# One PSUM bank for the up products of a delta-rule and feed-forward kernel, emptied by VectorE; two merges placed beside other pieces; last stores from two queues

## The chip, the cores and the metric

The kernel runs on one core of a Trainium2 chip. The metric is the device time of one execution in microseconds (us). Three runs of the kernel before gave 621.1, 622.01 and 622.45 us; the median is 622.01 us. One further execution was profiled: it took 620.85 us by its own timer, and the span from its first to its last instruction is 619.1 us, so 1.75 us lie outside the span.

## The reference

A linear attention with a state that follows the delta rule, over 768 steps for 4 batches of 8 heads of width 48, and then a feed-forward layer with a piecewise activation:

```python
for t in range(S):
    kt, vt, bt = (k_n[:, :, t], v[:, :, t], beta[:, :, t, None])
    y[:, :, t] = np.einsum('bhd,bhde->bhe', q[:, :, t], state)
    v_old = np.einsum('bhde,bhd->bhe', state, kt)
    state = state + bt[:, :, :, None] * np.einsum('bhd,bhe->bhde', kt, vt - v_old)
...
h = x @ w_in
g = np.where(pos, h, np.where(neg, 0.0, (h + beta) ** 2 / (4.0 * beta)))
return (g @ w_out).astype(np.float32)
```

Here x is y with the heads side by side (3072 rows of 384), w_in is 384 x 2048, w_out is 2048 x 384, pos is h >= 1, neg is h <= -1 and beta is 1. So g is h above 1, 0 below -1, and a parabola between.

## The kernel before

**Tiling.** The 768 steps are cut into 12 chunks of 64, and two chunks of all four batches make a pair, G = 0 to 5, of 512 rows. Inside a chunk the delta rule is solved as a triangular system, and the state is carried from chunk to chunk. The feed-forward layer of a pair runs over 16 blocks f of 128 hidden units. One block of one pair is an *item*. Pair 0 is split further, so there are 102 items: 22 for pair 0, and 16 for each of the pairs 1 to 5.

**An item.** `up` (L628 to L637) makes 9 matmuls of 512 columns into a PSUM bank h: three slices of the contraction, each in three passes of high and low parts. The activation then goes over two engines. ScalarE computes relu(0.5 - 0.5 h) out of PSUM into s (L762), relu(1 - s) in place (L762 again, since both go through the helper `relu`) and its square (L789). VectorE takes the maximum of h, still in PSUM, and s (L791). `rest` (L753 to L759) splits s into ghi, a rounded copy by ScalarE (L757), and glo, the remainder, by VectorE (L758). `down` (L639 to L651) makes 12 matmuls of 384 columns into the four banks o0 to o3, two items later.

**PSUM.** The eight banks are two named h, which take turns item by item, two named ch, and o0 to o3. The attention's *pieces*, which are groups of 64 to 128 small matmuls, get their banks from `acc` (L65): in pairs 1 to 5 from the two ch banks alone.

**Order.** The order is written by hand. While the items of pair G run, the attention of pair G+1 is computed between them. `plan` (L687 onward) puts pieces (`pe`) and VectorE work (`fill`) into half-slots: half-slot t of a pair belongs to item floor(t), and a whole number stands just behind that item's `up`, a half one behind the `down` that follows it. Each engine works through its own instructions in exactly the order of the code. In the order of one item: what a piece of the half-slot before still has to move (`finish(late)`), `rest` of the item before, `up`, the first relu, the pieces and fills of the whole slot, `down` of two items earlier, the other ScalarE steps, the pieces of the half slot, the maximum, and the fills of the half slot.

**The attention of a pair.** `gram_k` (L204) and `gram_q` (L217) multiply keys with keys and queries with keys. The result of `gram_q` is masked by three VectorE instructions (L237). `lanes` (L264) transposes the key products and normalizes; GpSimd then masks A (L296). `solve_whole` (L319) inverts 32 x 32 triangles in 30 steps of two VectorE instructions each (L325, L327), which are fills of the items 0 to 7 and of the end of the pair before. `unlanes_whole` (L330) brings the result back (L333, L335, L338). `merge32` (L385) joins two triangles of 32 into one of 64, with matmuls L392 and L394 and six ScalarE copies. `chain_r`, `chain_u`, `chain_y` and `chain_d` (L409 to L513) go through the two chunks in turn and carry the state SU.

In pairs 1 to 4 `chain_r` of the first chunk stands at half-slot 2.5, `gram_q` of the first at 4.5 and of the second at 6, the merges at 8.5, 9 and 11 and the chain from 10 to 15. Pair 5 has no such work beside its items.

**The end.** `store` (L653) copies each bank o to SBUF and issues two DMAs of 96 KB for it; in the last pair ScalarE and VectorE copy in turn, and all but the last of the eight DMAs are issued by the SP queue.

Of the kernel before, what the change touches and what calls it, by code (L numbers as in the profile page):

```python
# [7 lines left out]
F32 = mybir.dt.float32  # L8
F32R = mybir.dt.float32r
I32 = mybir.dt.int32  # L10
AF = mybir.ActivationFunctionType
ALU = mybir.AluOpType

C = 64
NP = 4
D = 48
CT = 2
NV = CT * NP
DM = 384
# [11 lines left out]
def delta_rule_moe(ctx: ExitStack, tc: tile.TileContext, kqa, kqb, kv, beta, w, out):  # L31
# [14 lines left out]
    nc = tc.nc  # L46
    ntot, NT = kv.shape[0], kv.shape[1]
    CB = NT * CT
    NU = CB * NP
    H = NU // 2  # L50
    NB = CB * C
    P = 128
    NS = ntot // 2
    TT = 2 * NB // P

    const = ctx.enter_context(tc.tile_pool(name="const", bufs=1))
    sb = ctx.enter_context(tc.tile_pool(name="sb", bufs=2))
# [1 line left out]
    ctx.enter_context(tc.manual_schedule())  # L59

    K, KE, GE, Q, KV, XB, RAW, WT = {}, {}, {}, {}, {}, {}, {}, {}
    START = [dict(name=n, bufs=b) for n, b in (("ch", 2), ("ch", 2), ("h", 2), ("h", 2), ("o2", 1), ("o3", 1), ("o0", 1), ("o1", 1))]
    spare = []

    def acc():  # L65
# [151 lines left out]
    def gram_q(g):  # L217

        x, b_ = Q[g], banks(C)
        for j in range(H):  # L220
            for e, f in quarters():
                r, o = slice(f * C, f * C + D), other(e, f) * C
                nc.tensor.matmul(b_[e][o:o + C, j], K[g][r, e * H + j, :], x[r, (1 - f, 1)[e], e * H + j, :], start=True, stop=True)  # L223

        def moved():
            for o in range(2):
                yield x[o * C:o * C + C, o, 0:H], b_[0][o * C:o * C + C], slice(o * C, o * C + C)
            yield x[:, 0, H:NU], b_[1], slice(0, P)

        def evict():  # L230
            def raw():
                for a, b, r in moved():
                    nc.scalar.copy(out=a, in_=b)

            def masks(copied=False):
                for a, b, r in moved():
                    nc.vector.tensor_tensor(out=a, in0=a if copied else b, in1=mask[r, None, :].broadcast_to([r.stop - r.start, H, C]), op=ALU.mult)  # L237
                    yield
            return (raw, masks(True)) if g < 2 else lambda: run(masks())
        return evict  # L240
# [373 lines left out]
    oacc, gs = {}, {}  # L614
# [13 lines left out]
        return slice(bs[0] * NB, bs[-1] * NB + NB)  # L628

    def up(G, f, bs):  # L630
        h = ps.tile([P, 2 * NB], F32, name="h", bufs=2)
        n = 0
        for k in range(3):
            for x, y in PASSES:
                nc.tensor.matmul(h[:, cols(bs)], WT[f][:, 0, x, k * P:(k + 1) * P], XB[G][:, y, k, cols(bs)], start=(n == 0), stop=(n == 8))  # L635
                n += 1
        return h  # L637
# [15 lines left out]
    def store(G, b):  # L653
        o = sb.tile([P, 2, DM], F32, name="wx", bufs=2)
        for k in (2 * b, 2 * b + 1):
            (nc.scalar.copy, nc.vector.tensor_copy)[k % 2 if G == NS - 1 else 0](out=o[:, k % 2], in_=oacc[G, k])
            for j in range(CT):
                (nc.scalar if G == NS - 1 and k + j == TT else nc.sync).dma_start(out=out.rearrange("(b n t) m -> n b t m", b=CB, t=C)[2 * G + b, k % 2 * CT + j], in_=o[j * C:j * C + C, k % 2])

    pe, fill = {}, {}  # L660

    def at(where, G, t, *x):
        where.setdefault(2 * first[G] + int(round(2 * t)), []).extend(x)
# [5 lines left out]
    def chain(G, t, a):  # L669
        for j, f, g in ((0, chain_u, a), (0.5, chain_y, a), (1.5, chain_d, a), (2.5, chain_r, a + 1), (3.5, chain_u, a + 1), (4, chain_y, a + 1), (5, chain_d, a + 1)):  # L670
            if (f, g) != (chain_d, ntot - 1):
                at(pe, G, t + j, lambda f=f, g=g: f(g))

    def plan(G):

        a, b = 2 * G + 2, 2 * G + 3
        if G == NS - 1:
            return
        va, vb = scale_v(a), scale_v(b)
        if G == 0:  # L680
            for j, f in ((0, merge16_b), (0.5, chain_r), (1, lambda g: merge32(g, None, True)), (2, lambda g: merge32(None, g)), (3, chain_u), (4, chain_y), (5, chain_d)):
                at(pe, G, j, lambda f=f: f(1))
            back = restore()
            at(fill, G, 0, (sv[1], 2))
            at(fill, G, 1, (load_k, b), (weight_loads, 7, 9), (load_q, a), (weight_loads, 9, 10), (load_kv, a), (weight_loads, 10, 13))
            at(fill, G, 1.5, (back, 1))
            at(fill, G, 2.5, (back, 1), (raws[1][1], 9))  # L687
            for j, n in enumerate((2, 2, 3)):
                at(fill, G, 3.5 + j, (early[0], n))
            at(fill, G, 6.5, (early[1], 1))  # L690
            at(fill, G, 7, (early[1], 9))
            at(fill, G, 4.5, (load_q, b), (weight_loads, 13, 14))
            at(fill, G, 5.5, (load_kv, b), (weight_loads, 14, 15))
            at(fill, G, 8, (load_k, a + 2), (weight_loads, 15, FT))
            for j in range(2):
                at(fill, G, 6 + j / 2, (va, 1))
                at(fill, G, 11.5 + j / 2, (vb, 1))
            at(pe, G, 6, lambda: gram_q(a))
            at(pe, G, 7, lambda: chain_r(a))
            at(pe, G, 11, lambda: gram_q(b))  # L700
            for j, f in ((8, merge16_a), (9.5, merge16_b)):
                for g in range(2):
                    at(pe, G, j + g / 2, lambda f=f, g=g: f(g))
            M = 12.5
            last = FT + HALF
        else:
            so, un = solves.pop(G)
            at(fill, G, 0.5, (va, 1))
            at(fill, G, 1, (va, 1))
            at(pe, G, 2.5, lambda: chain_r(a))  # L710
            at(pe, G, 4.5, lambda: gram_q(a))
            at(pe, G, 6, lambda: gram_q(b))
            cost, hs = 0, 0
            t, n = (-2.5, 19) if G == 1 else (-1.5, 17)
            for j in range(1, 31):
                at(fill, G, t + hs / 2, (so, 1))
                cost += j * (31 - j) + 150
                hs = int(cost / 9461 * n)
            for j, t in enumerate((7, 7.5, 8, 8)):
                at(fill, G, t, (un, 1))  # L720
            at(fill, G, 9, (vb, 1))
            at(fill, G, 9.5, (vb, 1))
            M = 8.5
            last = 16
        for j, x in ((0, (0, None)), (0.5, (1, 0)), (2.5, (None, 1))):
            at(pe, G, M + j, lambda x=x: merge32(*x))
        chain(G, M + 1.5, a)
        if G < NS - 2:
            if G:
                at(fill, G, 6.5, (load_k, a + 2))  # L730
            at(fill, G, M + 0.5, (load_k, b + 2, (nc.sync, nc.sync), True))
            at(pe, G, M + 1, lambda: gram_k(a + 2))
            at(pe, G, M + 3.5, lambda: gram_k(b + 2))
            lane_steps(G, M + 2, lanes(G + 2), 2.5, 3, 3.5, 4)
            solves[G + 1] = solve_whole(), unlanes_whole()
            at(fill, G, M + 3, (load_q, a + 2))
            at(fill, G, M + 5, (load_k, b + 2))
            at(fill, G, M + 6.5, (load_q, b + 2))
            at(fill, G, last + 0.5, (load_kv, a + 2))
            at(fill, G, last + 1.5, (load_kv, b + 2))  # L740
# [20 lines left out]
    def relu(out, in_, bias, scale):  # L761
        nc.scalar.activation(out=out, in_=in_, func=AF.Relu, bias=bias, scale=scale)  # L762

    late, last, ready = [], None, []
    for n, item in enumerate(items):
        at_, c = 2 * n, cols(item[2])
        finish(late)
        if last:
            rest(*last)
            ready.append(last[0])  # L770
        if at_ == 2 * HALF:
            spare.clear()
        h = up(*item)

        s = sb.tile([P, 2 * NB], F32, name="s", bufs=2)
        relu(s[:, c], h[:, c], mid, -0.5)
        evicts = products(*pe.pop(at_, []))
        run(wu, 3 if n == 0 else 1)
        fills(at_)
        finish(evicts)  # L780
        run(wu, 2 if n < HALF else 1)
        if len(ready) == LAG:
            x = ready.pop(0)
            down(*x)
            for b in x[2]:
                if left[x[0], b] == 0:
                    store(x[0], b)
        relu(s[:, c], s[:, c], one, -1.0)
        nc.scalar.activation(out=s[:, c], in_=s[:, c], func=AF.Square)  # L789
        late = products(*pe.pop(at_ + 1, []))  # L790
        nc.vector.tensor_tensor(out=s[:, c], in0=h[:, c], in1=s[:, c], op=ALU.max)  # L791
        run(wu, 2)
        fills(at_ + 1)
        last = item, s
# [3 lines left out]
    for b in range(2):  # L798
        gs[G, FT - 1, (b,)] = gs[G, FT - 1, (0, 1)]
        down(G, FT - 1, (b,))  # L800
        store(G, b)

# [1 line left out]
def layouts(q, k, v, beta, moe_w_in, moe_w_out):  # L804
# [43 lines left out]
```

## Time and profile before

| | |
|---|---|
| median of three runs | 622.01 us |
| profiled execution, its own time | 620.85 us |
| its span | 619.1 us |
| items of pair 1 begin at | 188.9 us |
| items of pair 5 begin at | 541.0 us |
| ScalarE busy | 393.9 us (64%) |
| GpSimd busy | 29.8 us (5%) |
| granted TensorE clock from 120 to 600 us | 1.00 |

The pairs 0 to 4 and the preparation ahead of them fill the first 541 us. From pair 1 on, a pair with attention beside it takes about 90 us, and from the first to the last `up` of pair 5 there are 63 us. In the profile's rows PE is TensorE, DVE is VectorE, ACT is ScalarE, POOL is GpSimd; SPq and ACTq are the DMA issues of the SP and ScalarE queues. A row of the timeline has the start and the duration in us, then engine, line of the code and operation, what is written and read, the sizes, and in brackets how long the engine stood idle before and what ended that.

### The profile page before, as it was taken

The page shows a single profiled execution, that of the slowest core. Times are in us where ns is not written, and L with a number is a line of the kernel's source. Part 1 is how long each engine was busy: PE and PEld are TensorE (multiplying, and loading weights), DVE is VectorE, ACT ScalarE, POOL GpSimd, SP SyncE. Part 2 cuts the span into 40 slices and gives each one's busy share as a digit, 9 for nine tenths or more (in the row PEclk, how much of TensorE's full clock was granted, in tenths as well). Part 3 has the DMA queues.
Part 4 walks back from the last instruction along what each step waited for, and adds up shares of the span by engine and source line. Part 5 has one row for each costly group of instructions (what it writes and reads, how often), then busy time and mean ns, then how long its engine had stood idle before and what let it go on. Part 6 is the DMA issues. An engine that isn't in the chain of part 4 may idle for free.

```text
span 619.1 us, 21754 instructions
## 1 busy us (share of the span) xinstructions
PE 583.6 (94%) x9562; PEld 511.5 (83%) x9562; DVE 409.3 (66%) x848; ACT 393.9 (64%) x685; POOL 29.8 (5%) x62
## 2 busy tenths in 40 slices
PE   7977967799999999999999999999999999999996
PEld 7966956688888888888888888888888888889995
DVE  4989899972379873379973489954489945333332
ACT  3436775649667569656578646587647586666663
POOL 5110000010010000020000020000020000000000
PEclk9556697999999999999999999999999999999999
DMA  5672756200124210214210224110124000020002
GB/s 141 197 244 71 233 196 202 88 4 3 42 61 119 74 31 3 69 31 125 72 30 8 65 53 119 54 31 24 49 71 124 1 4 16 12 54 1 0 1 51
DMA packets 32831, 42.97 MB, mean 69 GB/s; under 512 B 7152, under 2 KB 27440, under 8 KB 32736
## 3 DMA queue, kind: packets, MB, share of 16 engines
q1 hardware_dynamic: 31600, 39.43, 22.6%
q10 hardware_dynamic: 880, 2.07, 1.0%
q8 instruction: 75, 1.23, 0.8%
q0 software_dynamic: 256, 0.08, 0.1%
q14 instruction: 20, 0.16, 0.1%
HBM read 34.47 MB, written 4.72 MB: 63 GB/s over the span
## 4 chain that ended last, share of the span: by engine, by line
PE 70%; ACT 11%; DVE 9%; SPq 3%; DMA 3%; issue 2%; DVEq 0%; ACTq 0%
PE o L650 27%; PE h L635 27%; PE ch L452 3%; ACT XT L406 2%; ACT GG L404 2%; PE ch L414 2%; ACT s L762 2%; PE ch L223 2%; PE ch L430 1%; ACT XT L399 1%; PE ch L496 1%; PE o L583 1%; PE ch L375 1%; ACT s L789 1%; SPq L484 1%
## 5 line engine op out<-in xcount | busy, mean ns | idle before, releaser
L635 PE MATMUL h<-xb,wt 128*128 128x512 f32 (+1 forms) x918 | 229.1, 395 | 9.1 <-DMA xb<-wt 8.1
L635 PEld LDWEIGHTS h<-xb,wt 128*128 128x128 f32 x918 | 166.8, 195 | 43.2 <-DVE xb L183 4.4
L650 PE MATMUL o<-wt,ghi 128*128 128x384 f32 x768 | 202.1, 344 | 0.1
L791 DVE TENSOR_TENSOR s<-h,s 128x512 f32<-128x512 f32 (+1 forms) x102 | 66.8, 655 | 124.3 <-ACT s L789 123.8
L650 PEld LDWEIGHTS o<-wt,ghi 128*128 128x128 f32 x768 | 137.8, 189 | 7.5 <-issue 0.5
L757 ACT CAST ghi<-s 128x512 fp32r<-128x512 f32 (+1 forms) x102 | 60.8, 597 | 110.4 <-DVE s L791 86.3
L650 PE MATMUL o<-wt,glo 128*128 128x384 f32 x384 | 130.3, 339 | 0.4 <-DVE glo L758 0.3
L762 ACT ACTIVATE s<-h,half 128x512 f32<-128x512 f32 (+1 forms) x102 | 67.5, 662 | 44.6 <-PE h L635 43.7
L758 DVE TENSOR_TENSOR glo<-s,ghi 128x512 fp32r<-128x512 f32 (+1 forms) x102 | 66.6, 653 | 34.9 <-ACT ghi L757 34.8
L650 PEld LDWEIGHTS o<-wt,glo 128*128 128x128 f32 x384 | 72.7, 189 | 1.0 <-DVE glo L758 1.0
L762 ACT ACTIVATE s<-s,one 128x512 f32<-128x512 f32 (+1 forms) x102 | 71.7, 703 | 2.4
L789 ACT ACTIVATE s<-s 128x512 f32<-128x512 f32 (+1 forms) x102 | 61.9, 607 | 3.2
L325 DVE TENSOR_TENSOR pr<-A 128x30 f32<-128x30 f32 (+14 forms) x120 | 39.3, 328 | 6.2 <-POOL A L296 4.5
L327 DVE TENSOR_TENSOR A<-A,pr 128x30 f32<-128x30 f32 (+14 forms) x120 | 39.9, 332 | 4.4
L452 PEld LDWEIGHTS ch<-Q,SU 64*64 64x64 f32 (+1 forms) x1008 | 22.1, 135 | 4.3 <-ACT ghi L757 1.5
L452 PE MATMUL ch<-Q,SU 64*64 64x64 f32 (+1 forms) x1008 | 24.3, 222 | 0.7 <-ACT SU L434 0.7
L237 DVE TENSOR_TENSOR Q<-ch,mask 64x512 f32<-64x512 f32 (+1 forms) x30 | 20.6, 688 | 0.4
L296 POOL TENSOR_SCALAR_AFFINE_SELECT A<-A 128x1024 f32<-128x1024 f32 x4 | 5.1, 1263 | 311.9 <-DMA xb<-X 258.1
L404 ACT ACTIVATE GG<-ch 32x512 f32<-32x512 f32 x22 | 13.0, 589 | 10.6 <-PE ch L392 10.3
L414 PEld LDWEIGHTS ch<-SU,K 48*64 48x64 f32 x672 | 13.2, 147 | 6.5 <-issue 4.6
L414 PE MATMUL ch<-SU,K 48*64 48x48 f32 x672 | 14.9, 232 | 3.7 <-DVE Q L237 3.7
L179 ACT ACTIVATE xb<-wt 128x768 f32<-128x768 f32 x16 | 14.5, 914 | 5.1 <-DVE wt L191 3.6
(150 smaller groups left out, 621.8 us busy)
## 6 DMA issues: line engine op xcount, KB each, us to landing
wt<-in_w_dram SPq DMA_DIRECT2D x14, 768.0 KB, 5.4
out_dram<-wx SPq DMA_DIRECT2D x47, 96.0 KB, 2.2
KV<-in_kv_dram SPq DMA_DIRECT2D x36, 96.0 KB, 2.5
KV<-in_kv_dram SPq DMA_DIRECT2D x72, 48.0 KB, 2.4
KV<-in_kv_dram SPq DMA_DIRECT2D x12, 192.0 KB, 2.7
xb<-X SPq DMA_DIRECT2D x60, 32.0 KB, 2.0
K<-in_kqb_dram SPq DMA_DIRECT2D x12, 128.0 KB, 2.7
Q<-in_kqb_dram SPq DMA_DIRECT2D x12, 128.0 KB, 2.7
```

The costliest lines, as they stand in the source:

```text
L325: nc.vector.tensor_tensor(out=pr, in0=A[:, 0:n, j:j + 1].broadcast_to([P, n, m]), in1=A[:, j:j + 1, j + 1:32].broadcast_to([P, n, m]), op= ...
L327: nc.vector.tensor_tensor(out=A[:, 0:n, j + 1:32], in0=A[:, 0:n, j + 1:32], in1=pr, op=ALU.add)
L404: nc.scalar.mul(out=GG[r:r + 32, ga, :, 0:32], in_=y1[r:r + 32], mul=-1.0)
L414: nc.tensor.matmul(b_[f][o:o + C, j], K[g][r, k, :], SU[r, (1 - f, 1)[e], k, :], start=True, stop=True)
L452: nc.tensor.matmul(yy[i][o * C:o * C + C, e, p], SF[rows, u:u + C], w_[rows, x, k, :], **how)
L635: nc.tensor.matmul(h[:, cols(bs)], WT[f][:, 0, x, k * P:(k + 1) * P], XB[G][:, y, k, cols(bs)], start=(n == 0), stop=(n == 8))
L650: nc.tensor.matmul(oacc[G, k], (ghi, glo)[x][:, k * P:(k + 1) * P], WT[f][:, 1, y, :], start=(new and n == 0), stop=(left[G, b] == 0 and n ...
L757: nc.scalar.copy(out=ghi[:, c], in_=s[:, c])
L758: nc.vector.tensor_tensor(out=glo[:, c], in0=s[:, c], in1=ghi[:, c], op=ALU.subtract)
L762: nc.scalar.activation(out=out, in_=in_, func=AF.Relu, bias=bias, scale=scale)
L789: nc.scalar.activation(out=s[:, c], in_=s[:, c], func=AF.Square)
L791: nc.vector.tensor_tensor(out=s[:, c], in0=h[:, c], in1=s[:, c], op=ALU.max)
```

## The change

Up to pair 0 all stays as it was, apart from the banks' names: h becomes h0 and h1. From pair 1 on `up` writes to h0 alone. VectorE at once moves max(h, -1) into s in SBUF, a new instruction (L792 of the new code). ScalarE then computes q = relu(0.5 - 0.5 s) and (1 - q) squared, two steps in place of three, and the maximum (L815) reads s and q from SBUF. For s = max(h, -1) the value 0.5 - 0.5 s never exceeds 1, so that the second relu isn't needed. From item 2 of pair 1 on, the bank h1 is a third bank for the pieces.

`gram_q` of the second chunk goes from half-slot 6 to 8.5, behind the first merge. The last merge goes from 11 to 10.5, ahead of `chain_y`. In the last pair the eight stores are issued by the SP queue and the ScalarE queue, four each.

```diff
     def up(G, f, bs):
-        h = ps.tile([P, 2 * NB], F32, name="h", bufs=2)
+        h = ps.tile([P, 2 * NB], F32, name="h0" if G else f"h{f % 2}")
...
+    def send(G, k, j, o, q):
+        q.dma_start(out=out.rearrange("(b n t) m -> n b t m", b=CB, t=C)[2 * G + k // 2, k % 2 * CT + j], in_=o[j * C:j * C + C, k % 2])
+
+    def store_last(G):
+        o = [sb.tile([P, 2, DM], F32, name="wx", bufs=2) for _ in range(2)]
+        for k in range(TT + 1):
+            if k < TT:
+                (nc.scalar.copy, nc.vector.tensor_copy)[k % 2](out=o[k // 2][:, k % 2], in_=oacc[G, k])
+                send(G, k, 0, o[k // 2], nc.sync)
+            for x in ((0,), (), (1,), (), (2, 3))[k]:
+                send(G, x, 1, o[x // 2], nc.scalar)
...
             at(pe, G, 4.5, lambda: gram_q(a))
-            at(pe, G, 6, lambda: gram_q(b))
...
-        for j, x in ((0, (0, None)), (0.5, (1, 0)), (2.5, (None, 1))):
+        for j, x in ((0, (0, None)), (0.5, (1, 0)), (2 if G else 2.5, (None, 1))):
             at(pe, G, M + j, lambda x=x: merge32(*x))
+        if G:
+            at(pe, G, M, lambda: gram_q(b))
...
+        if item[:2] == (1, 2):
+            spare[:] = START[0:2] + [dict(name="h1", bufs=1)]
         h = up(*item)
 
         s = sb.tile([P, 2 * NB], F32, name="s", bufs=2)
-        relu(s[:, c], h[:, c], mid, -0.5)
+        if item[0]:
+            nc.vector.tensor_scalar(out=s, in0=h, scalar1=-1.0, scalar2=None, op0=ALU.max)
+            q = sb.tile([P, 2 * NB], F32, name="A16", bufs=1)
+            relu(q, s, mid, -0.5)
+        else:
+            relu(s[:, c], h[:, c], mid, -0.5)
...
-        relu(s[:, c], s[:, c], one, -1.0)
-        nc.scalar.activation(out=s[:, c], in_=s[:, c], func=AF.Square)
+        if item[0]:
+            nc.scalar.activation(out=q, in_=q, func=AF.Square, bias=one, scale=-1.0)
+        else:
+            relu(s[:, c], s[:, c], one, -1.0)
+            nc.scalar.activation(out=s[:, c], in_=s[:, c], func=AF.Square)
         late = products(*pe.pop(at_ + 1, []))
-        nc.vector.tensor_tensor(out=s[:, c], in0=h[:, c], in1=s[:, c], op=ALU.max)
+        if item[0]:
+            nc.vector.tensor_tensor(out=s, in0=s, in1=q, op=ALU.max)
+        else:
+            nc.vector.tensor_tensor(out=s[:, c], in0=h[:, c], in1=s[:, c], op=ALU.max)
```

**VectorE, pair 3, from glo of item 5 to glo of item 6.** Line, operation, what is written and read, and the size; glo belongs to the item before the one whose fills follow it. Before:

```order
L758 TENSOR_TENSOR glo<-s,ghi 128x512
L325 TENSOR_TENSOR pr<-A 128x108
L327 TENSOR_TENSOR A<-A,pr 128x27x4
L325 TENSOR_TENSOR pr<-A 128x84
L327 TENSOR_TENSOR A<-A,pr 128x28x3
L237 TENSOR_TENSOR Q<-ch,mask 64x512 x2
L237 TENSOR_TENSOR Q<-ch,mask 128x512
L791 TENSOR_TENSOR s<-h,s 128x512
L325 TENSOR_TENSOR pr<-A 128x58
L327 TENSOR_TENSOR A<-A,pr 128x29x2
L325 TENSOR_TENSOR pr<-A 128x30
L327 TENSOR_TENSOR A<-A,pr 128x30
```

The same place now (L771 is glo, L792 the new move, L815 the maximum, A_6189 is q):

```order
L771 TENSOR_TENSOR glo<-s,ghi 128x512
L792 TENSOR_SCALAR s<-h_6177 128x512
L325 TENSOR_TENSOR pr<-A 128x108
L327 TENSOR_TENSOR A<-A,pr 128x27x4
L325 TENSOR_TENSOR pr<-A 128x84
L327 TENSOR_TENSOR A<-A,pr 128x28x3
L815 TENSOR_TENSOR s<-s,A_6189 128x512
L325 TENSOR_TENSOR pr<-A 128x58
L327 TENSOR_TENSOR A<-A,pr 128x29x2
L325 TENSOR_TENSOR pr<-A 128x30
L327 TENSOR_TENSOR A<-A,pr 128x30
```

The move of item 6 now stands behind glo of item 5 and ahead of the solve steps of its slot, and the three masks of `gram_q` have left this slot. Nothing else of VectorE's work has moved here.

**VectorE, pair 3, items 8 and 9 now.** These are the rows into which the masks have gone:

```order
L338 STREAM_TRANSPOSE GG<-XT 128x16x32 x2
L815 TENSOR_TENSOR s<-s,A_6274 128x512
L237 TENSOR_TENSOR Q<-ch,mask 64x512 x2
L237 TENSOR_TENSOR Q<-h_6325,mask 128x512
L771 TENSOR_TENSOR glo<-s,ghi 128x512
L792 TENSOR_SCALAR s<-h_6372 128x512
L258 TENSOR_TENSOR KV<-KV,N_5675 128x384
```

The masks stand between the maximum of item 8 and its glo, so that the move of item 9 is behind all of them.

**ScalarE, the end of the program now.** The rows after the last ghi (L770); L667 is the copy of a bank o, L661 a store:

```order
L770 CAST ghi<-s 128x512
L667 COPY wx<-o_8425 128x384
L661 DMA out_dram<-wx 64x384
L667 COPY wx<-o_8433 128x384
L661 DMA out_dram<-wx 64x384 x3
```

ScalarE issues one store between its two copies and three behind them; before, it made both copies and then issued a single store.

More of the change, by code (lines that the diff above doesn't have):

```diff
@@ L61, in delta_rule_moe @@
     K, KE, GE, Q, KV, XB, RAW, WT = {}, {}, {}, {}, {}, {}, {}, {}
-    START = [dict(name=n, bufs=b) for n, b in (("ch", 2), ("ch", 2), ("h", 2), ("h", 2), ("o2", 1), ("o3", 1), ("o0", 1), ("o1", 1))]
+    START = [dict(name=n, bufs=b) for n, b in (("ch", 2), ("ch", 2), ("h0", 1), ("h1", 1), ("o2", 1), ("o3", 1), ("o0", 1), ("o1", 1))]
     spare = []
@@ L655, in store @@
         for k in (2 * b, 2 * b + 1):
-            (nc.scalar.copy, nc.vector.tensor_copy)[k % 2 if G == NS - 1 else 0](out=o[:, k % 2], in_=oacc[G, k])
+            nc.scalar.copy(out=o[:, k % 2], in_=oacc[G, k])
             for j in range(CT):
-                (nc.scalar if G == NS - 1 and k + j == TT else nc.sync).dma_start(out=out.rearrange("(b n t) m -> n b t m", b=CB, t=C)[2 * G + b, k % 2 * CT + j], in_=o[j * C:j * C + C, k % 2])
+                send(G, k, j, o, nc.sync)
+    def send(G, k, j, o, q):
[8 more added lines that the diff above has]
+                send(G, x, 1, o[x // 2], nc.scalar)
     pe, fill = {}, {}
@@ L800, in delta_rule_moe @@
         down(G, FT - 1, (b,))
-        store(G, b)
+    store_last(G)
 def layouts(q, k, v, beta, moe_w_in, moe_w_out):
```

## The prediction

> **What bounds the kernel now.** First the busy shares, then the slices of the span (40 of 15.5 us each, one digit for each tenth busy), then the busy time in three stretches: items 0 to 7 of pair 3, items 8 to 15 of it, and pair 5.
>
> ```profile
> PE 583.6 (94%) x9562; PEld 511.5 (83%) x9562; DVE 409.3 (66%) x848; ACT 393.9 (64%) x685; POOL 29.8 (5%) x62
> PE   7977967799999999999999999999999999999996
> DVE  4989899972379873379973489954489945333332
> 365.86:403.35 37.49, 37.49 (x361) 33.16 (x361) 35.73 (x86) 21.37 (x35) 1.04 (x2) 1.00 0.33 88
> 403.35:455.44 52.09, 51.81 (x1065) 44.43 (x1065) 26.43 (x52) 38.18 (x69) 2.47 (x4) 1.00 0.13 34
> 545.86:604.27 58.41, 58.41 (x295) 52.88 (x295) 19.37 (x28) 38.81 (x61) 0.00 (x0) 1.00 0.06 14
> ```
>
> In a row of stretches come the bounds and the length, then PE, weight loads, DVE, ACT, POOL, the granted clock and the DMA share. TensorE is the bound from pair 1 on: it has no idle time to speak of. VectorE's 66% is an average over two kinds of stretch: in items 0 to 7 it is busy for 35.73 of 37.49 us, in pair 5 for 19.37 of 58.41. In the first kind it has no room either, as its timeline shows:
>
> ```profile
> 363.21 1.26 POOL L296 TENSOR_SCALAR_AFFINE_SELECT A<-A 128x1024 f32<-128x1024 f32 x1 [85.80 <-DMA xb<-X]
> 364.51 0.19 DVE L325 TENSOR_TENSOR pr<-A 128x30 f32<-128x30 f32 x1 [1.50 <-POOL A L296]
> 365.98 0.69 DVE L758 TENSOR_TENSOR glo<-s,ghi 128x512 fp32r<-128x512 f32 x1
> 378.12 0.69 DVE L791 TENSOR_TENSOR s<-h,s 128x512 f32<-128x512 f32 x1 [0.30 <-ACT s L789]
> 396.97 0.68 DVE L758 TENSOR_TENSOR glo<-s,ghi 128x512 fp32r<-128x512 f32 x1
> 397.57 0.26 DVE L325 TENSOR_TENSOR pr<-A 128x108 f32<-128x108 f32 x1
> 397.87 0.27 DVE L327 TENSOR_TENSOR A<-A,pr 128x108 f32<-128x108 f32 x1
> 398.62 0.68 DVE L237 TENSOR_TENSOR Q<-ch,mask 64x512 f32<-64x512 f32 x1
> ```
>
> From 364.51, when GpSimd releases it, to 398.62 VectorE waits for another engine only once, 0.30 us at 378.12. The rest of its idle time is some 0.03 us between a solve step's two instructions (397.57 + 0.26 to 397.87), which depend on each other and leave room for nothing. Two banks h let it lag behind TensorE, and it does. So here both engines are full, and an instruction more on VectorE is paid for if TensorE has to wait for it.
>
> **What a full item and a piece cost TensorE.** The starts of `up` of items 6, 7 and 8 of pair 3:
>
> ```profile
> 393.72 2.25 PE L635 MATMUL h<-xb,wt 128*128 128x512 f32 x9
> 395.90 1.16 PE L223 MATMUL ch<-Q,K 48*64 48x64 f32 x64
> 399.19 2.24 PE L635 MATMUL h<-xb,wt 128*128 128x512 f32 x9
> 403.35 2.24 PE L635 MATMUL h<-xb,wt 128*128 128x512 f32 x9
> ```
>
> Item 7 without a piece takes 403.35 - 399.19 = 4.16 us, item 6 with `gram_q` 5.47, so the piece costs 1.31.
>
> **The new move: its duration.** The trace has no one-source VectorE instruction from PSUM of 512 columns. The nearest rows:
>
> ```profile
> 612.18 0.56 DVE L656 COPY wx<-o 128x384 f32<-128x384 f32 x1 [1.06 <-PE o L650]
> L791 DVE TENSOR_TENSOR s<-h,s 128x512 f32<-128x512 f32 x90 | 61.8, 687 | 118.1 <-ACT s L789 117.8
> L181 DVE TENSOR_SCALAR xb<-xb 128x768 int32<-128x768 int32 x16 | 9.1, 566 | 0.0
> L185 DVE SCALAR_TENSOR_TENSOR xb<-wt,xb 128x768 int32<-128x768 int32 x16 | 15.2, 953 | 0.3
> ```
>
> A two-source instruction of 512 columns takes 0.687 us; back to back, as 396.97 to 397.57 above, it holds VectorE for 0.60. A one-source copy out of PSUM of 384 columns takes 0.56, which is as slow as two sources, since 0.687 x 384/512 is 0.52. On the other side the one-source L181 in SBUF takes 0.566 for 768 columns against 0.953 with two sources: by that ratio 0.41, less the 0.09 of overlap some 0.3. So the ends are 0.3 and 0.69; I take 0.60, since the copy out of PSUM is the nearest row. The Trainium skill, "VectorE: DVE Perf Modes", section "Why PSUM operands drop a tier", says that the doubled rate needs both SBUF read ports and that PSUM has a single one, so that fp32 out of PSUM runs at single rate; the copy's row agrees, and by that rule the low end falls away and the sum stays.
>
> **Where it stands.** The move of item n is queued behind glo of item n-1 and ahead of item n's fills. `up` of item n+1 now waits for it. Behind it are the solve steps, all masks and maxima, and through them ScalarE's ghi and TensorE's `down`.
>
> **Term 1, items 0 to 8 of the pairs 2, 3 and 4: +4.6 us each.** Worked out in pair 3. Between the release at 364.51 and the place of item 6's move, 397.57, the moves of items 15 (of the pair before) and 0 to 5 are new, and item 6's own: 8 x 0.60 = 4.8. The move of item 14 delays the normalization ahead of the GpSimd step, for 0.60 less the 0.18 idle there now:
>
> ```profile
> 359.86 0.49 DVE L479 TENSOR_TENSOR X<-ch,X 128x128 fp32r<-128x128 f32 x2 [0.18 <-issue]
> ```
>
> That adds 0.4; the 0.30 at 378.12 is used up. The move of item 6 ends at 397.57 + 4.8 + 0.4 - 0.3 = 402.5. TensorE alone would begin `up` of item 7 at 399.19 - 1.31 = 397.9, as `gram_q` is gone from item 6. It waits for 4.6 us in all, spread over the items. The masks are taken off VectorE only behind this move, so their 2.1 us help nothing ahead of it. From item 7 on VectorE is under TensorE: items 7 and 8 hold 3.1 and 4.7 us of old work on it, plus 0.6 each, against 4.16 and, with two pieces in item 8, 6.7. So the 4.6 us stay, and nothing after gives them back. Pairs 2 and 4 have the same instructions in a stretch as full (bounds and length, then VectorE):
>
> ```profile
> 275.00:317.30 42.30, 40.16 (x93) 1.00 0.31 80
> 454.00:496.50 42.50, 40.27 (x93) 1.00 0.27 69
> ```
>
> Three pairs: **13.8 us**.
>
> The Trainium skill, "Perfetto Trace Analysis", section "Optimizing Scalar/DVE Operations", advises to hand work from a saturated VectorE to ScalarE. The change does the opposite, and the rows above, with VectorE full, agree with the advice. Its fixed cost for VectorE on PSUM, about 125 ns, with 512 columns at the 0.96 GHz of "VectorE: DVE Perf Modes" gives an estimate of 0.66 us; with that in place of 0.60 the sum below would be 1.8 us longer.
>
> **Term 2, pair 1: +2.0 us.** It has the same steps, but only the moves of items 0 to 6 are new (the items of pair 0 keep the old way), and VectorE has two longer waits:
>
> ```profile
> 201.91 0.69 DVE L791 TENSOR_TENSOR s<-h,s 128x512 f32<-128x512 f32 x1 [0.55 <-ACT s L789]
> 209.85 0.69 DVE L791 TENSOR_TENSOR s<-h,s 128x512 f32<-128x512 f32 x1 [0.62 <-ACT s L789]
> 217.57 0.26 DVE L325 TENSOR_TENSOR pr<-A 128x108 f32<-128x108 f32 x1
> 220.06 2.24 PE L635 MATMUL h<-xb,wt 128*128 128x512 f32 x9
> ```
>
> 217.57 + 7 x 0.60 - 0.55 - 0.62 = 220.6, against 220.06 - 1.31 = 218.75 for TensorE.
>
> **Term 3, the merges and the chain: +1.0 us in all.** Here ScalarE is nearly full, and TensorE waits a little for it:
>
> ```profile
> 408.73:424.30 15.57, 15.29 (x401) 12.92 (x395) 4.35 (x8) 14.50 (x25) 0.00 (x0) 1.00 0.10 28
> 414.51 0.32 PE L210 MATMUL ch<-K 48*64 48x64 f32 x2
> 415.00 1.15 PE L210 MATMUL ch<-K 48*64 48x64 f32 x62 [0.17 <-ACT GG L404]
> 417.65 1.07 ACT L214 COPY GG<-ch 128x512 f32<-128x512 f32 x2
> 418.61 0.63 ACT L757 CAST ghi<-s 128x512 fp32r<-128x512 f32 x1
> 419.13 0.70 ACT L762 ACTIVATE s<-h,half 128x512 f32<-128x512 f32 x1
> 421.24 0.73 ACT L762 ACTIVATE s<-s,one 128x512 f32<-128x512 f32 x1
> ```
>
> ScalarE is busy for 14.50 of 15.57 us in items 9 and 10. The change takes 0.73 us an item from it (the row at 421.24). But its first relu followed ghi at once (418.61, 419.13), and now it waits for the move, which waits for glo, which waits for that ghi: 0.65 + 0.60 + 0.1 = 1.35 us. So ScalarE loses about 0.6 an item where it is full. `gram_k` at 414.51 stands still from its second matmul to 415.00, some 0.4 us, until ScalarE has emptied a bank; the third bank doesn't help, as two come from the merge just before. Its copies will be 0.6 later in the item, so the wait grows to about 1.0. Against that, the last merge ahead of `chain_y` covers the 0.2 us for which that waits for SU. And pieces that follow each other spare a change of tile size, some 0.1 twice. I put it at +0.3 in pairs 1 to 3 and nothing in pair 4, which has no `gram_k`. The bounds are -0.6 for each pair, if both waits vanish, and +1.3, if ScalarE's 0.6 in both items is paid in full.
>
> **Pair 5: nothing.** VectorE goes from 19.37 us to 19.37 + 14 x 0.6 in 58.41; the move of an item has the 2.1 us of a `down` to end in.
>
> **Term 4, the end: -1.7 us.**
>
> ```profile
> 612.16 4.40 SPq L658 DMA_DIRECT2D out_dram<-wx  x7
> 612.84 0.34 PE L650 MATMUL o<-wt,glo 128*128 128x384 f32 x1
> 613.22 0.56 DVE L656 COPY wx<-o 128x384 f32<-128x384 f32 x1 [0.48 <-PE o L650]
> 613.81 0.56 ACTq L658 DMA_DIRECT2D out_dram<-wx  x1
> ```
>
> The last bank is in SBUF at 613.78, but SP, at 0.63 us a store, issues until 616.56, and the span ends 2.5 us after that. Now SP issues four, to 614.7, and ScalarE its last three from 613.2 at 0.56, to 614.9: 1.7 us earlier.
>
> **Sum.** 13.8 + 2.0 + 1.0 - 1.7 = +15.1 us. The profiled execution took 620.85, which gives 636.0; the median of the runs is 1.2 above it, so **637**.
>
> **The rivals.**
>
> *Faster: the moves find room.* If VectorE's moves cost TensorE nothing, what is left is the end's 1.7 and the waits of 0.6 in four pairs, 4.1 in all: 618 by the median. The room before item 7 of pair 3 is 397.9 - 397.57 + 0.3 = 0.6 us; for this case eight moves must fit into it, under 0.08 us each. All rows of VectorE above speak against it. 7%.
>
> *A cheap read.* At 0.37 us a move, near the SBUF end, pair 3 gets 397.57 + 0.2 + 8 x 0.37 - 0.3 = 400.4, +2.5, pair 1 +0.2; with 1.0 and -1.7 the sum is +7.2: 629. The 0.56 of the copy speaks against it. 12%.
>
> *The relay through VectorE bounds the chain too.* ScalarE's 0.6 an item is paid in items 9 and 10 of the four pairs, 1.3 each in place of 0.3: +4.3 on the sum, 641. For it speaks ScalarE's 14.50 of 15.57; against it that TensorE waits there for only two of its results. 19%.
>
> **How the numbers follow.** The forecast has 62%: 637, and by itself 631 to 643. The range of 625 to 645 leaves out the faster case, and of the others what lies beyond the unknown costs: moves at 0.3 with no loss in the chain give about 623, moves at 0.69 whose waits for ScalarE aren't used up, with the chain at its worst, some 649. A measurement of this kernel tells about 0.2% from no change. Faster by more than that: 8%; within: 3%; slower: 89%.
>
> **What would show it.** L792 near 0.69 us in 80 instructions; TensorE waiting for VectorE ahead of `up` in items 0 to 7 of the pairs 1 to 4, in sum about 16 us, and not in pair 5; item 7 of pair 3 beginning 4.6 us later counted from item 14 of pair 2; the last store issued before 615 us plus the shift. It would be wrong if L792 took under 0.4 us, if items 0 to 7 took no longer, or if the chain's items became shorter.

## The result, and the profile after

The changed kernel takes 662.77 us in the median (660.29 to 663.25), the kernel before 621.91 in the runs beside it: a ratio of 1.0641 with a 95% interval of 1.0614 to 1.0668, so 41 us slower. Forecast were 637 us and a range up to 645. The direction was right, and the loss is 2.7 times the one worked out. The profiled execution has a span of 661.5 us, 42.4 more than before.

From the page of the changed kernel, the busy shares, the slices and the head of the chain that ended last:

```profile
PE 601.1 (91%) x9562; PEld 517.9 (78%) x9562; DVE 459.8 (70%) x928; ACT 347.4 (53%) x605; POOL 30.0 (5%) x62
DVE  4889899852599864589964589974589965444443
DVE 36%; PE 32%; ACT 18%; issue 6%; DMA 4%; SPq 2%; POOL 1%; ACTq 0%; DVEq 0%; POOLq 0%
```

VectorE has its 80 instructions more, ScalarE its 80 fewer. The chain that ended last is 36% VectorE's and 18% ScalarE's; before, TensorE had 70% of it, VectorE 9% and ScalarE 11%. But VectorE isn't full: it is busy for 70% of the span, against 66% before. Where such a chain goes through an engine that is not full, it is made of hand-overs. The same stretches as before the change, items 0 to 7 and 8 to 15 of pair 3 and pair 5 (bounds and length, then PE, weight loads, DVE, ACT, POOL, granted clock):

```profile
390.14:431.15 41.01, 39.12 (x297) 33.05 (x297) 37.65 (x89) 17.94 (x28) 0.00 (x0) 0.96 0.28 75
431.15:488.02 56.87, 52.97 (x1129) 45.49 (x1129) 34.67 (x65) 32.34 (x60) 3.50 (x6) 1.00 0.13 35
586.10:646.96 60.86, 60.55 (x295) 52.07 (x294) 27.80 (x42) 29.30 (x45) 0.00 (x0) 1.00 0.06 14
```

The first two are longer, the first although `gram_q` of the second chunk has gone from it to the second, and although VectorE has more idle time there than before (37.65 of 41.01 against 35.73 of 37.49). And pair 5, for which the prediction gave nothing, has gone from 58.41 to 60.86 us, while VectorE is busy for 27.80 us of it. That is the place to look, since nothing but the items' own work runs there. Two items of pair 5, VectorE's and ScalarE's rows of the timeline, then TensorE's of the same stretch:

```profile
628.89 0.68 DVE L792 TENSOR_SCALAR s<-h 128x512 f32<-128x512 f32 x1
631.18 0.69 DVE L815 TENSOR_TENSOR s<-s,A 128x512 f32<-128x512 f32 x1 [1.61 <-ACT A L809]
632.62 0.69 DVE L771 TENSOR_TENSOR glo<-s,ghi 128x512 fp32r<-128x512 f32 x1 [0.74 <-ACT ghi L770]
633.23 0.68 DVE L792 TENSOR_SCALAR s<-h 128x512 f32<-128x512 f32 x1
```

```profile
629.67 0.72 ACT L775 ACTIVATE A<-s,half 128x512 f32<-128x512 f32 x1 [1.42 <-DVE s L792]
630.42 0.72 ACT L809 ACTIVATE A<-A,one 128x512 f32<-128x512 f32 x1
631.96 0.62 ACT L770 CAST ghi<-s 128x512 fp32r<-128x512 f32 x1 [0.81 <-DVE s L815]
634.00 0.72 ACT L775 ACTIVATE A<-s,half 128x512 f32<-128x512 f32 x1 [1.42 <-DVE s L792]
```

```profile
629.63 2.34 PE L635 MATMUL h<-xb,wt 128*128 128x512 f32 x9
633.71 0.34 PE L650 MATMUL o<-wt,glo 128*128 128x384 f32 x1
633.96 0.96 PE L635 MATMUL h<-xb,wt 128*128 128x512 f32 x3
```

Read in order of time, this is a ring. The move at 628.89 releases the relu (629.67), that the square (630.42), that the maximum (631.18), that ghi (631.96), that glo (632.62), and behind glo in VectorE's order stands the next move (633.23). Its length is 633.23 - 628.89 = 4.34 us: 0.78 + 0.75 + 0.76 + 0.78 + 0.66 + 0.61. TensorE would need 4.14 to 4.20, as before the change. The matmuls that the next move empties, 629.63 to 631.97, have been over for 1.26 us when it starts. So from item 3 of pair 5 on every item is paced by the ring, at 4.33 to 4.34 us. TensorE's busy time of 60.55 us hides this: each `up` stands behind a wait of its weight loads for L792, 0.24 us for the one at 629.63, while the matmuls before it still count as busy.

The ring is worse where other work stands in it. In item 10 of pair 4, ScalarE's copies of SU stand behind the relu, and `chain_y` (L452) waits for them (TensorE's rows, then the granted clock in that piece):

```profile
543.99 1.15 PE L430 MATMUL ch<-KV,XT 64*64 64x48 f32 x64
550.46 3.66 PE L452 MATMUL ch<-Q,SU 112*64 112x64 f32 x96 [1.91 <-ACT SU L434]
```

```profile
547.92 0.68 DVE L792 TENSOR_SCALAR s<-h 128x512 f32<-128x512 f32 x1
```

```profile
550.00:554.00 4.00, 3.54 (x96) 3.41 (x96) 0.69 (x1) 2.54 (x5) 0.00 (x0) 0.57 0.02 4
```

The `up` of this item was over at 544.1, but its move starts at 547.92, behind a glo that had waited for ScalarE. After 1.91 us without work, TensorE's granted clock in the next 4 us is 0.57, and the piece takes 3.66 us where it took 2.28 before. The item takes 12.2 us. Before the change it took 8.5, without the merge that now stands in it; with the merge, in the first experiment below, it takes 8.8.

### The profile page after: what moved, and what is told of

Same layout as the page of the kernel before. It is cut to its first block, busy times and chain, and to the rows that moved or that the text cites. A ratio compares the mean times of both kernels' runs of the same rounds, so it can differ in the third digit from the quotient of the medians.

```text
span 661.5 us, 21870 instructions
## 1 busy us (share of the span) xinstructions
PE 601.1 (91%) x9562; PEld 517.9 (78%) x9562; DVE 459.8 (70%) x928; ACT 347.4 (53%) x605; POOL 30.0 (5%) x62
## 4 chain that ended last, share of the span: by engine, by line
DVE 36%; PE 32%; ACT 18%; issue 6%; DMA 4%; SPq 2%; POOL 1%; ACTq 0%; DVEq 0%; POOLq 0%
PE h L635 13%; PE o L650 10%; DVE glo L771 5%; DVE s L792 5%; ACT A L775 4%; ACT A L809 4%; DVE s L815 3%; DVE pr L325 3%; DVE A L327 2%; DVE Q L237 2%; ACT ghi L770 2%; PE ch L452 2%; DMA K<-in_kqa_dram 1%; DVE SU L511 1%; DVE XT L335 1%
## 5 line engine op out<-in xcount | busy, mean ns | idle before, releaser
L635 PE MATMUL h<-xb,wt 128*128 128x512 f32 (+1 forms) x918 | 239.2, 407 | 28.6 <-DVE s L792 16.3
L635 PEld LDWEIGHTS h<-xb,wt 128*128 128x128 f32 x918 | 169.3, 200 | 74.3 <-DVE s L792 21.5
L650 PE MATMUL o<-wt,ghi 128*128 128x384 f32 x768 | 202.4, 345 | 1.2 <-ACT ghi L770 0.8
L775 ACT ACTIVATE A<-s,half 128x512 f32<-128x512 f32 x80 | 57.9, 724 | 159.9 <-DVE s L792 153.8
L815 DVE TENSOR_TENSOR s<-s,A 128x512 f32<-128x512 f32 x80 | 55.4, 692 | 98.6 <-ACT A L809 98.3
L770 ACT CAST ghi<-s 128x512 fp32r<-128x512 f32 (+1 forms) x102 | 60.8, 596 | 86.3 <-DVE s L815 47.9
L771 DVE TENSOR_TENSOR glo<-s,ghi 128x512 fp32r<-128x512 f32 (+1 forms) x102 | 66.6, 653 | 24.7 <-ACT ghi L770 24.6
L809 ACT ACTIVATE A<-A,one 128x512 f32<-128x512 f32 x80 | 58.2, 727 | 2.0
L792 DVE TENSOR_SCALAR s<-h 128x512 f32<-128x512 f32 x80 | 54.8, 685 | 4.4 <-PE h L635 4.4
L452 PE MATMUL ch<-Q,SU 64*64 64x64 f32 (+3 forms) x768 | 23.3, 232 | 1.9 <-ACT SU L434 1.9
L817 DVE TENSOR_TENSOR s<-h,s 128x256 f32<-128x256 f32 (+1 forms) x22 | 11.9, 541 | 17.9 <-ACT s L812 17.7
L452 PEld LDWEIGHTS ch<-Q,SU 64*64 64x64 f32 (+3 forms) x768 | 21.0, 144 | 3.8 <-ACT SU L434 2.2
L775 ACT ACTIVATE s<-h,half 128x256 f32<-128x256 f32 (+1 forms) x22 | 12.5, 570 | 12.9 <-PE h L635 12.8
```

What stands on the lines that cost most here:

```text
L452: nc.tensor.matmul(yy[i][o * C:o * C + C, e, p], SF[rows, u:u + C], w_[rows, x, k, :], **how)
L650: nc.tensor.matmul(oacc[G, k], (ghi, glo)[x][:, k * P:(k + 1) * P], WT[f][:, 1, y, :], start=(new and n == 0), stop=(left[G, b] == 0 and n ...
L770: nc.scalar.copy(out=ghi[:, c], in_=s[:, c])
L771: nc.vector.tensor_tensor(out=glo[:, c], in0=s[:, c], in1=ghi[:, c], op=ALU.subtract)
L792: nc.vector.tensor_scalar(out=s, in0=h, scalar1=-1.0, scalar2=None, op0=ALU.max)
L809: nc.scalar.activation(out=q, in_=q, func=AF.Square, bias=one, scale=-1.0)
```

## The experiments

Times are medians; each ratio is against the kernel before, run on the same chip.

### The move ahead of glo

The changed kernel, with VectorE's move of item n ahead of ghi and glo of item n-1 in the code. VectorE has the same instructions, and on ScalarE ghi still stands ahead of the relu, so that only VectorE's order differs.

```diff
         if last and not item[0]:
             rest(*last)
             ready.append(last[0])
...
         if item[0]:
             nc.vector.tensor_scalar(out=s, in0=h, scalar1=-1.0, scalar2=None, op0=ALU.max)
+            rest(*last)
+            ready.append(last[0])
             q = sb.tile([P, 2 * NB], F32, name="A16", bufs=1)
```

> As the changed kernel, but VectorE makes the move of item n ahead of glo of item n-1 in place of behind it. Ring theory: the move waits for glo, glo for ghi, ghi for the maximum, the maximum for the square and the relu, and these for the move before; six steps of about 0.7 us with their hand-overs are 4.34 us, more than the 4.17 that TensorE needs for an item. With the move ahead of glo the ring is open: the items of pair 5 go back from 4.34 to 4.17-4.19 us, and of the 41 us that the change lost some 10 to 20 come back, to about 642-652 us; items 0 to 7 of pairs 2 to 4 still lose 4 to 5 us a pair to the eight moves. Work theory (VectorE has 0.6 us more per item, whatever the order): within 3 us of the changed kernel's 662.8, and pair 5 stays at 4.34.

Measured: 634.02 us, ratio 1.0203 (1.018 to 1.0226). So 28.7 of the 41 us come back by a change of order alone, more than expected. Pair 5 of this kernel, VectorE's, ScalarE's and TensorE's rows in order of time:

```profile
599.34 2.24 PE L635 MATMUL h<-xb,wt 128*128 128x512 f32 x9
600.54 0.62 ACT L770 CAST ghi<-s 128x512 fp32r<-128x512 f32 x1 [0.81 <-DVE s L817]
601.62 0.69 DVE L792 TENSOR_SCALAR s<-h 128x512 f32<-128x512 f32 x1 [1.17 <-PE h L635]
602.23 0.68 DVE L771 TENSOR_TENSOR glo<-s,ghi 128x512 fp32r<-128x512 f32 x1
603.50 0.86 PE L635 MATMUL h<-xb,wt 128*128 128x512 f32 x3
```

The move now waits for TensorE (1.17 us), and no longer TensorE for the move; the item takes 4.16 us (599.34 to 603.50). So the move's place behind glo cost most of the loss. In pair 5 that is the ring as it was read step by step; in the other pairs the steps weren't added up item by item. The work theory alone, which is the prediction's, falls for those 28.7 us, but describes what is left (below).

### The new way in pair 5 alone

The kernel before, with the single bank and the move only for items with `item[0] == NS - 1`.

> The kernel before, with the single bank and VectorE's move in pair 5 alone, where no solve steps and no pieces stand beside the items; banks, pieces and stores as before. Ring theory: 14 or 15 items of 4.34 in place of 4.17 us and some 1.2 us more until the last ghi: 625 to 626 us. Work theory: VectorE has 30 us of idle time in pair 5, so nothing changes: 622 us within 0.5.

Measured: 626.27 us, ratio 1.0074 (1.0055 to 1.0093): 4.5 us more. From item 3 on, items of pair 5 take 4.33 to 4.34 us, and from the start of the last `up` to the end of the span there are 16.1 us in place of 14.8. VectorE is busy for 27.79 of the 60.77 us of items 1 to 14, so its work cannot be the reason; that the single bank is not the reason either, the runs with ScalarE below show.

### The last stores alone

The kernel before with `store_last` in place of the two calls of `store` at the end.

> The kernel before with the last eight stores issued by two queues, four each, and nothing else. By the prediction's term 4 the time falls by 1.7 us, to about 620.2; if the end is set by the landing of the last bank's own store and not by the queue, it falls by under 0.5 us.

Measured: 620.25 us against 621.79, ratio 0.998 (0.9966 to 0.9994); in the trace, the last `up` to the end takes 13.4 us in place of 14.8, 1.4 us less. Term 4 of the prediction holds, a little smaller: ScalarE takes 1.91 us to issue its last three stores, where three times 0.56 was assumed.

### ScalarE empties the bank

The changed kernel, but ScalarE makes t = relu(h + 1) out of PSUM, and VectorE takes max(t - 1, q) in one instruction, so that VectorE has two instructions an item, and ScalarE four, as before the change.

```diff
-            nc.vector.tensor_scalar(out=s, in0=h, scalar1=-1.0, scalar2=None, op0=ALU.max)
+            relu(s, h, one, 1.0)
             q = sb.tile([P, 2 * NB], F32, name="A16", bufs=1)
-            relu(q, s, mid, -0.5)
+            relu(q, s, one, -0.5)
...
-            nc.vector.tensor_tensor(out=s, in0=s, in1=q, op=ALU.max)
+            nc.vector.scalar_tensor_tensor(out=s, in0=s, scalar=-1.0, in1=q, op0=ALU.add, op1=ALU.max)
```

> As the changed kernel with its single bank, third bank for pieces, moved pieces and last stores, but ScalarE empties the bank: t = relu(h + 1), then q = relu(1 - 0.5 t) and (1 - q) squared, and VectorE takes max(t - 1, q) in one instruction. ScalarE has four instructions per item as before the change, VectorE two as before. If all the loss comes from the move on VectorE (its work, or the ring through glo): 617 to 621 us, no slower than before. If a single bank is itself too few, because up has to wait for whichever engine empties it: pair 5 above 4.25 us an item and the total above 625 us.

Measured: 622.61 us, ratio 1.0016 (1.0 to 1.0032). The 40 us are gone with VectorE's move, and pair 5 takes 4.14 to 4.21 us an item, from item 1 on, on a single bank. But the 1 to 5 us of gain did not come: item 0 of pair 3 takes 5.76 us in place of 4.23. There ScalarE's first step stands behind ghi of item 15, which waits for a late maximum, and `up` of item 1 waits 1.40 us for that step.

### ScalarE's first step ahead of ghi

The same, with that step of item n ahead of `rest` of item n-1, as in the first experiment.

```diff
             relu(s, h, one, 1.0)
+            rest(*last)
+            ready.append(last[0])
```

> As e4_scalar_empties, but ScalarE's first step of item n stands ahead of ghi of item n-1. In e4 items 0 of pairs 2 to 5's predecessors lose about 1.5 us: there ScalarE's first step waits behind ghi of item 15, which waits for a late maximum of VectorE, and up of item 1 waits for the bank. Queue theory: with the step ahead of ghi item 0 goes back to about 4.25 us, item 9 of pair 4 too, and the time falls by 5 to 7 us against e4, to 615.5 to 618 us, below the kernel before (621.8) by the last stores' 1.5 us and by about 1 us a pair in items 8 to 10. Bank theory (a single bank is too few for the hand-over at a pair's start): within 1 us of e4's 622.6.

Measured: 618.82 us, ratio 0.9949 (0.9931 to 0.9968). This version is 44 us below the changed kernel and 3.2 below the one before, a gain of half a per cent that lies clear of the interval. Item 0 of pair 3 takes 4.74 us, so not all of the 1.5 us came back, and the time is a little above the forecast range. Two items of pair 5 in its trace, ScalarE's rows and one of VectorE's:

```profile
583.72 0.69 ACT L775 ACTIVATE s<-h,one 128x512 f32<-128x512 f32 x1 [1.59 <-PE h L635]
584.31 0.61 ACT L770 CAST ghi<-s 128x512 fp32r<-128x512 f32 x1
584.95 0.69 DVE L771 TENSOR_TENSOR glo<-s,ghi 128x512 fp32r<-128x512 f32 x1 [2.09 <-ACT ghi L770]
587.88 0.69 ACT L775 ACTIVATE s<-h,one 128x512 f32<-128x512 f32 x1 [1.59 <-PE h L635]
```

The engine that empties the bank waits for TensorE (1.59 us), and what it does next no longer stands in the way of that. The Trainium skill, "Perfetto Trace Analysis", section "Optimizing Tensor Performance", asks for matmul groups to rotate through banks, so that the emptying of one overlaps the matmuls of the next. In pair 5 a single bank for `up` suffices: what follows an `up` directly is a `down` of 2.1 us, which goes to other banks, as the rule asks, and covers the 0.69 us of the emptying. In the full stretches the version still pays a little (the table below).

### The pieces in their old places

The changed kernel, and the version just above, with `gram_q` of the second chunk at 6 and the last merge at 11 again.

> The changed kernel with gram_q of the second chunk at 6 and the last merge at 11 again, single bank, move and third bank as they are. If the moved pieces are a part of the loss: below 660 us. If they gain about 1 us a pair, as items 9 and 10 of e4 show against before, or the moved masks relieve VectorE: 664 to 670 us, against 662.8 of the changed kernel.

> As e5_scalar_first with the pieces in their old places, gram_q at 6 and the last merge at 11. What e5 gains over this one is what the third bank is used for: about 1 us in each of four pairs, so 3 to 5 us slower than e5; if the moved pieces gain nothing, equal to e5 within 1 us.

Measured: 669.96 us (ratio 1.0779, 1.075 to 1.0807) and 622.45 us (1.0006, 0.9991 to 1.0021). The moved pieces gain 7.2 us in the changed kernel and 3.6 in the version with ScalarE. So this part of the change does what it is made for. The second run also has the quicker last stores, worth 1.5 us, and is still no faster than the kernel before: what else is new in it, the single bank among it, costs about as much as the stores gain. What the moved pieces would gain without the third bank is not shown; the first merge takes one bank and `gram_q` two, so two banks don't hold them beside each other.

### The work without the bank

The kernel before, with its two banks, and one more VectorE instruction per item from pair 1 on, whose result nothing waits for:

```diff
+        if item[0]:
+            q = sb.tile([P, 2 * NB], F32, name="A16", bufs=1)
+            z, zc = last[1], cols(last[0][2])
+            nc.vector.tensor_tensor(out=q[:, zc], in0=z[:, zc], in1=z[:, zc], op=ALU.max)
         evicts = products(*pe.pop(at_, []))
```

> The kernel before, with two banks and all else as it was, and one VectorE instruction more per item from pair 1 on, 512 columns in SBUF into a scratch tile, where the move stands: behind glo of item n-1. Nothing waits for its result, so that no ring closes and no bank hangs on it. Work theory: 0.6 us in each of some eight items of a full stretch, 4 to 5 us a pair in pairs 2 to 4, 2 to 3 in pair 1, nothing in pair 5: 634 to 640 us. If the two banks let VectorE lag so far that the work is hidden: below 627 us.

Measured: 642.44 us, ratio 1.0331 (1.0308 to 1.0355), 20.4 us more, 2.4 above the upper end of the forecast. Pair 5 keeps 4.14 to 4.20 us an item from item 1 on. So full stretches pay for VectorE's work with two banks too, at their start and their end: items 0, 7 and 8 of pair 3 take 5.81, 5.66 and 7.19 us in place of 4.23, 4.16 and 5.38. At the end TensorE waits 1.33 us for a maximum (L795 there) ahead of `up` of item 8, and 1.64 us for L335 ahead of the merge in it.

### Where the time is

Each length is the difference between the first matmuls of two `up` in the kernel's trace. The first row adds up items 0 to 8 of the pairs 1 to 4 and item 15 of the pairs 1 to 3, the second items 9 to 14 of the pairs 1 to 4, the third is the rest from item 15 of pair 4 on. All in us:

| | before | changed | move first | ScalarE first | extra work, two banks |
|---|---|---|---|---|---|
| full stretches | 185.6 | 217.5 | 202.2 | 186.9 | 202.4 |
| merges and chain | 162.3 | 169.3 | 159.6 | 159.5 | 166.4 |
| pair 5 and the end | 82.3 | 84.4 | 80.8 | 81.2 | 82.3 |

The changed kernel loses 31.9, 7.0 and 2.1 us. (The rest of the 42.4 us between the two spans, 1.4, lies ahead of pair 1, where the two kernels differ only in the banks' names: its items begin at 190.3 in place of 188.9, and in the traces of the experiments anywhere from 188.4 to 190.9.) The move's place behind glo, as the difference to the kernel with the move first, is 15.3 + 9.7 + 3.6 = 28.6 of that. What is left is 16.6 in the full stretches less 2.7 in the chain and 1.5 at the end.

## Why the prediction was right or wrong

**Where it failed.** The step is "Where it stands" and what was made of it. It says that the move of item n is queued behind glo of item n-1, and takes from that only what is queued behind the move. It didn't follow what glo itself waits for: ghi, the maximum, the square, the relu, and so the move of the item before. This closes a ring of 4.34 us that goes round once an item, longer where the solve steps, a square root or ScalarE's copies stand in it. Pair 5 was written down as nothing, because "the move of an item has the 2.1 us of a `down` to end in"; it has them, but it doesn't start until glo is done. Term 3 saw half of the ring (1.35 us through glo and the move) and priced it as a loss of ScalarE's time. The move ahead of glo, with all else equal, takes 28.7 us away, more than the whole gap of 25.8 between forecast and result. Without the ring the prediction's other terms are 4.65 + 4.59 + 4.60 + 2.7 - 2.7 - 1.5 = 12.3 us in the trace, and 12.2 in the medians, where 15.1 was summed.

**Term 1, VectorE's work: right for the kernel without the ring.** With the move first, items 0 to 8 of the pairs 2, 3 and 4, with the item 15 just ahead of each, lose 4.65, 4.59 and 4.60 us against before (for pair 3, 7.15 - 5.47 and 45.78 - 42.87), where 4.6 was worked out. In the changed kernel they lose 9.4, 8.2 and 7.9. The extra work with two banks costs the same items 5.0, 5.2 and 4.9 us, so the price is the work's and needs no single bank, though it falls partly in other items. One of the signs was written down wrongly: by the sum itself, item 7 of pair 3 should begin 402.5 - 399.19 = 3.3 us later, not 4.6, because `gram_q` has left item 6. Counted from item 14 of pair 2 it begins 6.4 us later in the changed kernel, and 3.4 with the move first.

**Term 2, pair 1: +2.7 with the move first, forecast +2.0.** About right; its own sum, 220.6 - 218.75, gives 1.85. In the changed kernel it is 6.4.

**Term 3, merges and chain: wrong in sign once the ring is gone.** It gives -2.7 us in four pairs with the move first, in place of +1.0. The gain is in items 10 and 11 together, into which the last merge was moved: 0.6 us less in each of the pairs 1 to 3, and 0.95 in pair 4. The prediction had given this move 0.2 us and 0.1 twice. Item 9, which was to get longer, is 0.41 and 0.13 us longer in the pairs 1 and 2, but 0.49 shorter in pair 3. How much of this is the merge's place, ScalarE's lost step or the third bank is not shown. In the changed kernel itself the stretch loses 7.0 us. The rival that had ScalarE's relay pay there priced it at 5.2 (four times 1.3), so it came near in this stretch, but its total of 641 us lacks what the full stretches and pair 5 lose.

**Term 4, the end: right in size.** The stores alone gain 1.5 us of time, 1.7 forecast. In the changed kernel most of it is taken back, since the last item's results come later: from the last `up` to the end there is a gain of 0.3 us, and the last store is issued by 658.7 us, where the sign allowed 615 plus the shift of the last `up`, 42.7.

**The duration of the move: right.**

```profile
L792 DVE TENSOR_SCALAR s<-h 128x512 f32<-128x512 f32 x80 | 54.8, 685 | 4.4 <-PE h L635 4.4
L635 PE MATMUL h<-xb,wt 128*128 128x512 f32 (+1 forms) x918 | 239.2, 407 | 28.6 <-DVE s L792 16.3
```

It takes 0.685 us, as much as a two-source instruction (0.687), and holds VectorE for 0.60 when the next instruction is ready (378.35 to 378.95 below), which is the value that the sum used. The Trainium skill, "VectorE: DVE Perf Modes", section "Why PSUM operands drop a tier", has fp32 out of PSUM at single rate; these rows agree, and the cheap read is refuted. The sign that was named, TensorE waiting for L792 ahead of `up`, is there with 16.3 us where about 16 was named. That this number fits is luck: the forecast meant VectorE's work, while the 16.3 include waits of the ring, and only as far as they show on the matmuls; the kernel lost 41 us. The waits also stand in pair 5, where they were not to be.

**The wait ahead of the solve: 0.4 forecast, more in fact.** In item 14 of pair 2 the square root stands behind the relu on ScalarE:

```profile
378.35 0.69 DVE L792 TENSOR_SCALAR s<-h 128x512 f32<-128x512 f32 x1
378.95 0.19 DVE L285 COPY N<-A 128x32 f32<-128x32 f32 x1
379.13 0.72 ACT L775 ACTIVATE A<-s,half 128x512 f32<-128x512 f32 x1 [2.05 <-DVE N L285]
379.76 0.21 ACT L246 ACTIVATE y<-N 128x32 f32<-128x32 f32 x1
380.01 0.18 DVE L247 TENSOR_SCALAR r<-y 128x32 f32<-128x32 f32 x1 [0.88 <-ACT y L246]
```

VectorE's wait for it is 0.88 us in place of 0.30. Item 15 of pair 2 takes 8.61 us here, 7.15 with the move first and 5.47 before; how much of that this wait makes up is not shown.

## What to carry to other kernels

When an instruction is put into an engine's order, follow not only who stands behind it but what the instruction ahead of it waits for, back through all engines, until the chain ends or comes back to the same instruction of the step before; if it comes back, the sum of its steps is the least time that a step can take, however idle the engines are. Where a step has a single bank, as here, the instruction that frees it belongs ahead of those that wait for results of the step before. And a stretch in which the engine has much idle time, such as pair 5 here, is where such a ring shows most clearly, since the engine's own work can't explain a longer step.

## What the runs showed of the hardware

A wait on TensorE can be paid twice. After 2.71 us without work ahead of item 0 of pair 2, the granted clock of the changed kernel is 0.83 over the next 10 us, and the nine matmuls take 3.37 us in place of 2.25:

```profile
289.91 3.37 PE L635 MATMUL h<-xb,wt 128*128 128x512 f32 x9 [2.71 <-DVE s L792]
290.00:300.00 10.00, 10.00 (x42) 8.63 (x42) 9.46 (x23) 4.04 (x6) 0.00 (x0) 0.83 0.42 116
```

It doesn't follow every such wait: in the changed kernel with the pieces in their old places, a wait of 2.72 us at the same item was followed by a granted clock of 1.00 over 10 us and nine matmuls in 2.35 us. What decides between the two isn't shown. The item took 5.83 us in the one and 5.84 in the other, so here the slower matmuls were hidden: VectorE was busy for 9.46 of the 10 us. In item 10 of pair 4, above, the slower piece cost 1.4 us more. From pair 1 on the mean granted clock is 0.98 in the changed kernel and 1.00 before.
